# Two first blocks of a convolution and expert kernel brought in by VectorE products and TensorE sums, with the first loads in a new order

## The chip, the cores and the metric

The kernel runs on one core of one Trainium2 chip. The metric is the device time of one execution in microseconds, as the median over runs. The profile is one execution recorded by the hardware profiler; its span runs from the first to the last instruction.

## What is computed

The reference takes a sequence `x` of 2 x 4096 rows of 192 values and, for every row, 8 heads x 7 taps of weights. A softmax over the 7 taps weighs the row and its six predecessors; the result goes through two dense layers with a squared ReLU between them, and then through two more with `h * cos(h)` between them:

```python
w = exp(weight_gen - max); w = w / (sum(w) + 1e-09)          # over the 7 taps
out = einsum('bshk,bskhg->bshg', w, x_unf)                   # x_unf: 7 neighbouring rows, zeros ahead of a batch
h = np.maximum(out @ w_in, 0.0);  x2 = (h * h) @ w_out       # 192 -> 2048 -> 192
h = x2 @ w_in2;                   y  = (h * np.cos(h)) @ w_out2
```

All in fp32. The kernel splits each fp32 operand in a high and a low part (`hi`, `lo`) of a shorter format that TensorE multiplies fast, and adds three products.

## The kernel before, in words

**Tiling.** The 8192 rows are 16 blocks of 512. One block of one expert is 16 steps, one for each 128 of the 2048 hidden columns. A step has five first-layer matmuls of 512 columns (`first_product`, line 560, into a PSUM tile `h`, of which there are four), the nonlinearity and the split in `hi` and `lo` (`between`, lines 588 to 618), and five second-layer matmuls (`second_product`, lines 577 to 583, into `acc`), which come six steps later. 16 blocks, two experts, 16 steps each: 512 steps, 5120 such matmuls. The first two blocks of the first expert are interleaved: the first block goes `ALONE` steps by itself, then the steps of both alternate.

**The start.** Before the first step TensorE needs the first block's rows, weighed by the softmax, transposed and split, and the first expert's weights, split. `load_x(0)` (line 361) loads the first block in 128 partitions of ten rows (`xc`); the two first partitions, which reach ahead of the batch, come by two small loads, the others by a load of 62 partitions on SP's queue and one of 64 on ACT's. `softmax(0, 0, 1)` works on the weights `wgen` of this block. `first_x1` (line 469) multiplies rows and weights for one row in four at a time on VectorE (`product`, line 441, the tile `pr` of 7 taps x 192), sums the taps of the first 128 columns by seven matmuls with the identity, which also transpose (line 482), and those of the last 64 by three additions on VectorE (line 487, written to `twice`) and a transpose on TensorE (line 493). All other blocks go through `attend` (line 449: products on GpSimd, one reduction each on VectorE, line 454) and `x1` (line 500: a transpose on VectorE, then out to DRAM and back to finish it, then a split).

**The weights** of the first expert are converted in pieces by `weight` (line 274): a load, then operations on ACT, VectorE and GpSimd (lines 303 to 320) that rebuild the value exactly, and the split (lines 264 to 271). Pieces: `wiAhi`, `wiAlo` (first layer, first 128 of 192 rows), `wiB` (last 64) and `wo` (second layer).

**The order.** Nothing is issued where it is written. Each operation is put in a list with its possible engines and a cost, and `Order.issue` (line 112) lays the list out by due times and by its own guess of when data arrive (`SENT`, `RATE`, `SEEN` for loads; `since` keeps an operation from being placed too early). On the chip each engine then runs its instructions in that fixed order. `WARM` matmuls with the identity (line 700) run while TensorE would have nothing to do.

Of the kernel before, what the change touches and what calls it, by code (L numbers as in the profile page):

```python
# [10 lines left out]
F32 = mybir.dt.float32  # L11
F32R = mybir.dt.float32r
# [14 lines left out]
ALONE = 6  # L27
WARM = 16
# [27 lines left out]
class Order:  # L56
    WAIT = 0.14

    SENT, RATE, SEEN = 0.65, 360e3, 0.77
# [117 lines left out]
def conv_moe_kernel(  # L177
# [46 lines left out]
    def load(dst, out_fn, in_ap, size, key=None, reads=(), by=1e9, queue="sp"):  # L224
        op({queue: 0.45}, lambda e: eng[e].dma_start(out=out_fn(), in_=in_ap), reads=reads,
           writes=[(dst, key)], size=size, by=by)
# [47 lines left out]
    def weight(m, part, c0, n):  # L274
        name = f"{part}{m}_{c0}"
        by = -99.0 if m == c0 == 0 and part != "o" else 1e9
        if m == 0:
            order.since = 3.0 if by < 0 else 5.0
# [4 lines left out]
        if part == "a":  # L283
            cols = n
            load(raw, lambda: flat()[:, 0:2 * n], w_in[m][0:P, 2 * c0:2 * (c0 + n)], P * n * 8, by=by)
        elif part == "b":

            cols = n // 2
            ap = w_in[m][P:D, 2 * c0:2 * (c0 + n)].rearrange("d (j k c) -> k d j c", k=2, c=2 * P)
            for k in range(2):  # L290
                load(raw, lambda k=k: flat()[k * DB:(k + 1) * DB, 0:n].rearrange("d (j c) -> d j c", c=2 * P),
                     ap[k], DB * n * 4, key=k, by=by)
# [68 lines left out]
    def load_x(b):  # L361
# [10 lines left out]
        if b:  # L372
            load(t, lambda: flat(p0, P, 0), rows_of(p0, P), P * rows * D * 4, key="all")
        else:
            for n, q in enumerate(((p0, P // 2), (P // 2, P))):
                load(t, lambda q=q: flat(*q, 0), rows_of(*q), P // 2 * rows * D * 4, key=f"all{n}", by=-100.0,
                     queue="act" if n else "sp")
# [90 lines left out]

    def first_x1():
        t = [buf(ps, [P, N], F32, "h", 4, f"first{part}") for part in range(2)]  # L470
        for i in range(BS):
# [6 lines left out]
            there = lambda part, i=i: t[part].t.rearrange("d (p i) -> d i p", i=BS)[:, i]  # L478

            def taps(e, pr=pr, there=there):  # L480
                for k in range(K):
                    nc.tensor.matmul(there(0), lhsT=pr.t[:, k, 0:P], rhs=ident.t, start=k == 0, stop=k == K - 1)
            op({"pe": 0.24 * K}, taps, [ident, (pr, 0)], [(t[0], i)])

            def fold(e, pr=pr, twice=twice):
# [5 lines left out]
            op({"dve": dve(3 * DB) + 2 * dve(2 * DB)}, fold, [], [(pr, 1), twice])  # L491

            op({"pe": 0.24}, lambda e, twice=twice, there=there: nc.tensor.transpose(
                there(1), twice.t.rearrange("p q d -> p (q d)"), ident.t), [ident, twice], [(t[1], i)])
        for part in range(2):
            split((0, 0), part, t[part], True)

# [160 lines left out]
    for b in range(NB):  # L658
# [8 lines left out]
        when(ago(NF + 8), load_x, b)  # L667
        if b % CB == 0:
            c = b // CB
            if c == 1:  # L670
                when(ago(2 * NF - 6), load_g, c)
                when(ago(2 * NF - 9), softmax, c, 0, CB)
            else:
                n = 14 + 9 * c
                when(n, early_exp, c, 2.27 * n + START + 15)
                when(ago(2 * NF), late_softmax, c)
        when(ago(NF), attend, b)
# [16 lines left out]
    with tc.manual_schedule():  # L694
# [56 lines left out]
```

## Time and profile before

| | |
|---|---|
| median of 3 runs | 1278.64 us (1277.4 to 1281.92) |
| the profiled execution | 1277.48 us |
| its span, first to last instruction | 1274.5 us |
| TensorE's mean granted clock over the span | 0.981 |
| TensorE busy | 1196.8 us, 94% |
| ScalarE, VectorE, GpSimd busy | 83%, 71%, 43% |

The span is 3.0 us shorter than the execution's own time. Busy shares are means over a start in which weights are converted and a long steady part. In rows, PE is TensorE's matmuls, PEld its weight loads, DVE VectorE, ACT ScalarE, POOL GpSimd, and SPq or ACTq the instructions that issue DMAs; `L560` is a line of the kernel; the bracket at a row's end is idle time ahead of it and what ended it.

### The profile page before, as it was taken

What the parts mean: (1) busy time and instruction counts of PE and PEld (TensorE: products, weight loads), DVE (VectorE), ACT (ScalarE), POOL (GpSimd) and SP (SyncE); (2) the same over time, 40 slices, a digit from 0 to 9 for tenths busy, and PEclk for the clock granted to TensorE, in tenths of its full rate; (3) what the DMA queues carried; (4) which work ended last, traced back from release to release, by engine and by line L of the source; (5) the groups of instructions that cost most, each with busy time, mean ns of one, the idle gap of its engine ahead of it and who ended that gap; (6) DMA issues with size and microseconds to landing.
All of it is one profiled execution on the core that took longest, in us unless ns stands there. A gap on an engine that the chain in (4) does not pass through costs nothing.

```text
span 1274.5 us, 16270 instructions
## 1 busy us (share of the span) xinstructions
PE 1196.8 (94%) x5212; PEld 979.1 (77%) x5212; DVE 902.8 (71%) x1217; ACT 1054.9 (83%) x1992; POOL 551.2 (43%) x425
## 2 busy tenths in 40 slices
PE   4488999989999999999999999999999999999998
PEld 4367777778787887878788787878878888888886
DVE  5998879775958578585866758576674646777765
ACT  1486887869788797978879798888988979999996
POOL 3678465564615244260534526153332304444443
PEclk8689999999999999999999999999999999999999
DMA  4532435320212112021111202111020210111001
GB/s 115 154 96 67 133 109 166 113 69 21 80 30 69 25 31 79 10 72 31 56 46 28 74 9 69 34 37 27 24 47 9 54 30 13 30 30 30 13 7 19
DMA packets 91945, 68.67 MB, mean 54 GB/s; under 512 B 56020, under 2 KB 77268, under 8 KB 91860
## 3 DMA queue, kind: packets, MB, share of 16 engines
q1 hardware_dynamic: 91780, 67.16, 19.1%
q8 instruction: 40, 0.66, 0.2%
q10 hardware_dynamic: 80, 0.49, 0.2%
q14 instruction: 45, 0.37, 0.1%
HBM read 47.76 MB, written 19.86 MB: 53 GB/s over the span
## 4 chain that ended last, share of the span: by engine, by line
PE 50%; ACT 18%; DVE 14%; issue 5%; DMA 2%; POOL 1%; SPq 1%; DVEq 0%; ACTq 0%; POOLq 0%
PE h L560 25%; PE acc L579 5%; PE acc L577 5%; PE acc L578 5%; PE acc L582 5%; PE acc L583 5%; ACT hi L264 5%; DVE lo L271 4%; ACT rr L609 4%; ACT rr L610 4%; DVE g L612 2%; ACT kk L604 2%; DVE rr L607 2%; ACT g L598 2%; DVE at L454 1%
## 5 line engine op out<-in xcount | busy, mean ns | idle before, releaser
L271 POOL TENSOR_TENSOR lo<-g,hi 128x512 fp32r<-128x512 f32 x201 | 260.2, 1295 | 557.4 <-ACT hi L264 489.3
L271 DVE TENSOR_TENSOR lo<-g,hi 128x512 fp32r<-128x512 f32 x215 | 175.0, 814 | 157.1 <-ACT hi L264 147.5
L264 ACT ACTIVATE hi<-g 128x512 fp32r<-128x512 f32 x416 | 259.8, 625 | 1.9 <-DVE g L612 0.9
L607 DVE SCALAR_TENSOR_TENSOR rr<-kk,h 128x512 f32<-128x512 int32 x256 | 174.4, 681 | 90.0 <-ACT kk L604 90.0
L612 DVE TENSOR_TENSOR g<-h,rr 128x512 f32<-128x512 f32 x256 | 175.0, 684 | 38.6 <-POOL lo L271 26.8
L577 PE MATMUL acc<-hi,wo 128*128 128x512 f32 x512 | 200.3, 391 | 1.5 <-ACT wo L264 1.5
L578 PE MATMUL acc<-hi,wo 128*128 128x512 f32 x512 | 200.6, 392 | 1.0 <-DVE wo L271 1.0
L582 PE MATMUL acc<-lo,wo 128*128 128x512 f32 x512 | 200.4, 391 | 0.0
L579 PE MATMUL acc<-hi,wo 128*128 128x512 f32 x512 | 200.4, 391 | 0.0
L583 PE MATMUL acc<-lo,wo 128*128 128x512 f32 x512 | 200.2, 391 | 0.0
L594 ACT ACTIVATE rr<-h 128x512 f32<-128x512 f32 x256 | 150.7, 590 | 51.0 <-PE h L560 50.0
L609 ACT ACTIVATE rr<-rr 128x512 f32<-128x512 f32 x256 | 161.1, 629 | 27.7 <-DVE rr L607 27.4
L610 ACT ACTIVATE rr<-rr 128x512 f32<-128x512 f32 x256 | 161.2, 630 | 1.8
L604 ACT ACTIVATE kk<-h 128x512 int32<-128x512 f32 x256 | 151.1, 590 | 8.5 <-PE h L560 7.8
L598 ACT ACTIVATE g<-rr 128x512 f32<-128x512 f32 x160 | 100.7, 630 | 55.1 <-DVE lo L271 51.5
L441 POOL TENSOR_TENSOR pr<-xc,wgen_late 128x1344 f32<-128x1344 f32 x48 | 139.5, 2984 | 13.2 <-DVE at L454 11.8
L577 PEld LDWEIGHTS acc<-hi,wo 128*128 128x128 f32 x512 | 96.8, 189 | 22.1 <-ACT wo L264 1.9
L578 PEld LDWEIGHTS acc<-hi,wo 128*128 128x128 f32 x512 | 96.7, 189 | 21.6 <-DVE wo L271 1.3
L582 PEld LDWEIGHTS acc<-lo,wo 128*128 128x128 f32 x512 | 96.7, 189 | 20.3
L583 PEld LDWEIGHTS acc<-lo,wo 128*128 128x128 f32 x512 | 96.8, 189 | 20.1
L579 PEld LDWEIGHTS acc<-hi,wo 128*128 128x128 f32 x512 | 96.8, 189 | 20.0
L454 DVE TENSOR_REDUCE at<-pr 128x192 f32<-128x1344 f32 x60 | 92.3, 1539 | 0.0
(558 smaller groups left out, 2243.7 us busy)
## 6 DMA issues: line engine op xcount, KB each, us to landing
xc<-in_x_dram SPq DMA_DIRECT2D x14, 960.0 KB, 4.7
x2d<-x2a SPq DMA_DIRECT2D x16, 256.0 KB, 2.0
x<-x2d SPq DMA_DIRECT2D x32, 128.0 KB, 2.7
x<-x2d SPq DMA_DIRECT2D x16, 256.0 KB, 2.7
out_dram<-oa SPq DMA_DIRECT2D x64, 64.0 KB, 2.0
x1d<-xt SPq DMA_DIRECT2D x60, 64.0 KB, 1.8
x<-x1d SPq DMA_DIRECT2D x15, 256.0 KB, 2.7
x<-x1d SPq DMA_DIRECT2D x30, 128.0 KB, 2.6
```

What stands on the lines that cost most here:

```text
L264: nc.scalar.activation(out, in_, AF.Copy)
L271: eng[e].tensor_tensor(out=out, in0=in0, in1=in1, op=ALU.subtract)
L560: nc.tensor.matmul(h.t, lhsT=w.t[:, sl], rhs=v.t, start=n == 0, stop=n == len(ops) - 1)
L577: nc.tensor.matmul(o0.t, lhsT=w(0), rhs=hi.t, start=start, stop=False)
L578: nc.tensor.matmul(o1.t, lhsT=w(2), rhs=hi.t, start=start, stop=False)
L579: nc.tensor.matmul(o0.t, lhsT=w(1), rhs=hi.t, start=False, stop=False)
L582: nc.tensor.matmul(o1.t, lhsT=w(2), rhs=lo.t, start=False, stop=stop)
L583: nc.tensor.matmul(o0.t, lhsT=w(0), rhs=lo.t, start=False, stop=stop)
L607: op({"dve": dve(N)}, lambda e: nc.vector.scalar_tensor_tensor(out=r.t, in0=k.t, scalar=-TWO_PI, in1=h.t, op0=ALU.mult, op1=ALU.add), [k, ...
L609: op({"act": act(N)}, lambda e: nc.scalar.activation(r.t, r.t, AF.Abs), [], [r])
L610: op({"act": act(N)}, lambda e: nc.scalar.activation(r.t, r.t, AF.Sin, scale=-1.0, bias=math.pi / 2), [], [r], behind=exps if (b, f) == (0 ...
L612: op({"dve": dve(N)}, lambda e: nc.vector.tensor_tensor(out=g.t, in0=h.t, in1=r.t, op=ALU.mult), [h, r], [g])
```

## The change

Line numbers of the changed file stand about 30 higher from `between` on and a few higher before. What it does:

- The first block's load is one of 126 partitions on SP (and the two small ones); nothing of it is on ACT's queue.
- The three loads of the first weight pieces (`wiA` and `wiB` of the first columns) go on ACT's queue, behind the first exponential in ACT's order. The second block's load is recorded after the second half of the softmax, with `since` 6.5.
- The second block no longer goes through `attend` and `x1`: `second_slot` multiplies on VectorE and sums all 192 columns' taps by 14 matmuls with the identity, between steps of the first block; `second_x1` splits from PSUM (the last 64 rows twice, for both halves of the partitions).
- `ALONE` is 8 and not 6, `WARM` 26 and not 16; the planner's figures for loads and for the fold's cost are others.

```diff
-ALONE = 6
-WARM = 16
+ALONE = 8
+WARM = 26
...
-    SENT, RATE, SEEN = 0.65, 360e3, 0.77
+    SENT, RATE, SEEN = 0.75, 300e3, 0.8
...
+        early = dict(queue="act", behind=exps[:1], by=by) if by < 0 else {}
         if m == 0:
-            order.since = 3.0 if by < 0 else 5.0
+            order.since = 0.0 if by < 0 else 6.5
...
-        if b:
-            load(t, lambda: flat(p0, P, 0), rows_of(p0, P), P * rows * D * 4, key="all")
-        else:
-            for n, q in enumerate(((p0, P // 2), (P // 2, P))):
-                load(t, lambda q=q: flat(*q, 0), rows_of(*q), P // 2 * rows * D * 4, key=f"all{n}", by=-100.0,
-                     queue="act" if n else "sp")
+        if b == 1:
+            order.since = 6.5
+        load(t, lambda: flat(p0, P, 0), rows_of(p0, P), P * rows * D * 4, key="all", by=1e9 if b else -100.0)
+        order.since = 0.0
...
+    def second_slot(i):
+        if i == 0:
+            acc[0, 1] = [buf(ps, [P, N], F32, f"acc{part}", 2, f"second{part}") for part in range(2)]
+        t = acc[0, 1]
+        pr = sbuf([P, K, D], F32, "pr", 2, f"pr1_{i}")
+        product(1, i, pr, ways={"dve": dve(K * D)})
+        for part in range(2):
+            rows = slice(P, D) if part else slice(0, P)
+            op({"pe": 0.24 * K}, lambda e, pr=pr, rows=rows, there=slot(t[part], i): taps(
+                e, there(rows.stop - rows.start), pr, rows), [ident, pr], [(t[part], i)])
...
+        if b == 1:
+            for i in range(BS):
+                when(ALONE - 6 + i, second_slot, i)
+            when(ALONE - 2, second_x1)
+            continue
         when(ago(NF), attend, b)
         when(ago(10), x1, b)
...
         softmax(0, 1, CB)
+        load_x(1)
```

How the planner's order moves, at three places. **SP's queue at the start**, before and then in the change (`wgen` is the taps' weights, `xc` a block's rows, `wo_early` and `wiB_early` places in which the first raw weights are put):

```order
L225 DMA wgen_99<-in_weight_gen_dram 128x224
L225 DMA xc_101<-in_x_dram 62x1920
L225 DMA xc_101<-in_x_dram 1x768
L225 DMA xc_101<-in_x_dram 1x1536
L225 DMA wgen_99<-in_weight_gen_dram 128x224
L225 DMA xc_108<-in_x_dram 128x1920
L225 DMA wgen_112<-in_weight_gen_dram 128x224
L225 DMA wo_early<-in_moe_w_in_dram 128x512
```

```order
L225 DMA wgen_109<-in_weight_gen_dram 128x224
L225 DMA xc_111<-in_x_dram 126x1920
L225 DMA xc_111<-in_x_dram 1x768
L225 DMA xc_111<-in_x_dram 1x1536
L225 DMA wgen_109<-in_weight_gen_dram 128x224
L225 DMA wgen_117<-in_weight_gen_dram 128x224 x2
L225 DMA xc_134<-in_x_dram 128x1920
L225 DMA wo_early<-in_moe_w_in_dram 128x768
```

The first block's rows (`xc_101`, now `xc_111`) come as one load, and the first weight piece (`128x512`) has left this queue for ACT's.

**VectorE, from the first block's last fold to the first block's split**, before and then in the change (`at` is `attend`'s sum for the second block, `xlo_(0, 0)` the low part of the first block):

```order
L454 TENSOR_REDUCE at_200<-pr_0_174 128x192
L313 TENSOR_SCALAR wiB_early<-wo_early 128x256 x2
L487 TENSOR_TENSOR wo_early<-wo_early 128x3x64
L487 TENSOR_TENSOR wo_early<-wo_early 128x2x64
L487 TENSOR_TENSOR wo_early<-wo_early 128x128
L318 SCALAR_TENSOR_TENSOR wiB_early<-wiAlo_early,wiB_early 128x256 x2
L454 TENSOR_REDUCE at_200<-pr_1_198 128x192
L313 TENSOR_SCALAR wiB_early<-wo_early 128x384
L315 TENSOR_SCALAR wiAlo_early<-wiAlo_early 128x384
L271 TENSOR_TENSOR xlo_(0, 0)_224<-first_132,xhi_(0, 0)_203 128x512
```

```order
L491 TENSOR_TENSOR wo_early<-wo_early 128x3x64
L491 TENSOR_TENSOR wo_early<-wo_early 128x2x64
L491 TENSOR_TENSOR wo_early<-wo_early 128x128
L315 TENSOR_SCALAR wiB_early<-wo_early 128x256 x2
L320 SCALAR_TENSOR_TENSOR wiB_early<-wiAlo_early,wiB_early 128x256 x2
L402 TENSOR_REDUCE mx_1_214<-wgen_109 128x32
L271 TENSOR_TENSOR xlo_(0, 0)_216<-first_140,xhi_(0, 0)_202 128x512
```

The reductions of the second block and the next weight piece are gone from ahead of the first block's split.

**VectorE after the first tiles**, in the change (`pr_0_246` to `pr_2_308` are products of the second block, `lo_294` and `lo_327` the low parts of the first two steps):

```order
L441 TENSOR_TENSOR pr_0_246<-xc_134,wgen_109 128x1344
L271 TENSOR_TENSOR wiAlo_67<-wiB_early,wiAhi_65 128x384
L441 TENSOR_TENSOR pr_1_274<-xc_134,wgen_109 128x1344
L320 SCALAR_TENSOR_TENSOR wiB_early<-wiAlo_early,wiB_early 128x256
L271 TENSOR_TENSOR lo_294<-h_235,hi_276 128x512
L315 TENSOR_SCALAR wiB_early<-wo_early 128x384 x2
L441 TENSOR_TENSOR pr_2_308<-xc_134,wgen_109 128x1344
L320 SCALAR_TENSOR_TENSOR wiB_early<-wiAlo_early,wiB_early 128x384
L271 TENSOR_TENSOR lo_327<-h_249,hi_291 128x512
```

These products stood on GpSimd before; they now lie among the weights' operations on VectorE, between the first tiles.

## Rows read from the trace of the kernel before

**Rows 1.** The page: the span and the instructions in it.

```profile
span 1274.5 us, 16270 instructions
```

**Rows 2.** Timeline of PE: start, duration, instruction, idle time before it.

```profile
26.63 1.83 PE L482 MATMUL first<-ident,wo_early 128*128 128x128 f32 x14 [2.44 <-DVE wo_early L441]
...
45.66 0.79 PE L560 MATMUL h<-xlo_(0, 0)_224,wiAhi 128*128 128x512 f32 x1 [6.23 <-DVE wiB_early L318]
...
108.89 0.50 PE L560 MATMUL h<-xlo_(0, 1)_370,wiAhi 128*128 128x512 f32 x1 [1.56 <-DVE lo L271]
```

**Rows 3.** Chain of waits in order of time: start, length, what.

```profile
111.45 1.13 PE h L560 x5
```

**Rows 4.** Waits of PE, 0 to 120 us: total, times, longest.

```profile
PE first L482 <- DVE pr L441: 12.3, 1, 12.3
...
PE h L560 <- DVE wiB_early L318: 6.2, 1, 6.2
```

**Rows 5.** Windows: length, busy by engine, granted clock, DMA share, GB/s.

```profile
5.00:10.00 5.00, 1.94 (x17) 1.75 (x16) 0.63 (x2) 0.00 (x0) 0.00 (x0) 1.00 0.99 254
10.00:15.00 5.00, 0.00 (x0) 0.00 (x0) 0.00 (x0) 0.00 (x0) 0.00 (x0) 0.69 0.15 52
...
270.00:271.00 1.00, 1.00 (x6) 0.82 (x5) 1.00 (x3) 0.00 (x0) 1.00 (x2) 1.00 0.88 361
```

**Rows 6.** DMA issues: of 0 to 25 us, of 255 to 300 us, and the page's.

```profile
xc<-in_x_dram SPq DMA_DIRECT2D x1, 465.0 KB
...
xc<-in_x_dram SPq DMA_DIRECT2D x1, 945.0 KB
...
xc<-in_x_dram SPq DMA_DIRECT2D x14, 960.0 KB, 4.7
```

**Rows 7.** Timeline of the queues and of ACT, same columns as rows 2.

```profile
1.19 1.36 SPq L225 DMA_DIRECT2D xc<-in_x_dram  x3
3.83 0.39 ACT L404 ACTIVATE wgen<-wgen 128x224 f32<-128x224 f32 x1 [1.59 <-DVE wgen L403]
21.67 0.44 ACT L303 ACTIVATE wiAlo_early<-wo_early 128x256 f32<-128x256 f32 x1 [17.46 <-DMA wo_early<-in_moe_w_in_dram]
...
267.34 0.67 SPq L225 DMA_DIRECT2D xc<-in_x_dram  x2
```

**Rows 8.** Timeline of DVE and POOL at the start.

```profile
5.27 0.39 DVE L414 TENSOR_TENSOR wgen<-wgen,sx 128x224 f32<-128x224 f32 x1
17.61 3.03 DVE L441 TENSOR_TENSOR pr<-xc,wgen 128x1344 f32<-128x1344 f32 x2 [11.94 <-DMA xc<-in_x_dram]
25.02 5.39 DVE L441 TENSOR_TENSOR wo_early<-xc,wgen 128x1344 f32<-128x1344 f32 x2
25.24 7.67 POOL L441 TENSOR_TENSOR pr<-xc,wgen 128x1344 f32<-128x1344 f32 x2 [0.39 <-DVE wgen L414]
35.08 2.90 DVE L313 TENSOR_SCALAR wiB_early<-wo_early 128x256 uint32<-128x256 uint32 x2
```

**Rows 9.** One line's instructions, 0 to 110 us: duration ns min/median/max, first and last start.

```profile
L441 DVE TENSOR_TENSOR pr<-xc,wgen x2: 1550/1554/1559, 17.6 to 19.1; 128x1344 f32<-128x1344 f32 x2
L487 DVE TENSOR_TENSOR wo_early<-wo_early x6: 291/291/2715, 30.3 to 38.6; 128x128 f32<-128x128 f32 x4, 128x192 f32<-128x192 f32 x2
L313 DVE TENSOR_SCALAR wiB_early<-wo_early x14: 282/480/2702, 35.1 to 99.2; 128x384 uint32<-128x384 uint32 x11, 128x256 uint32<-128x256 uint32 x3
L318 DVE SCALAR_TENSOR_TENSOR wiB_early<-wiAlo_early,wiB_early x18: 411/559/981, 38.8 to 100.5; 128x384 uint32<-128x384 uint32 x12, 128x256 uint32<-128x256 uint32 x6
L454 DVE TENSOR_REDUCE at<-pr x6: 1535/1539/1544, 33.6 to 108.8; 128x192 f32<-128x1344 f32 x6
```

**Rows 10.** Timeline of DVE at the end of the first weights.

```profile
96.73 2.84 DVE L313 TENSOR_SCALAR wiB_early<-wo_early 128x384 uint32<-128x384 uint32 x2
...
108.16 0.68 DVE L271 TENSOR_TENSOR lo<-h,hi 128x512 fp32r<-128x512 f32 x1
```

**Rows 11.** Windows of PE: length, busy (matmuls), granted clock, DMA share, GB/s.

```profile
250.00:270.00 20.00, 14.91 (x57) 0.91 0.11 36
```

More of the change, by code (lines that the diff above doesn't have):

```diff
@@ L222, in const, with load @@
         return Buf(None, tile=sb.tile(shape, dtype, name=name))
-    def load(dst, out_fn, in_ap, size, key=None, reads=(), by=1e9, queue="sp"):
+    def load(dst, out_fn, in_ap, size, key=None, reads=(), by=1e9, queue="sp", behind=None):
         op({queue: 0.45}, lambda e: eng[e].dma_start(out=out_fn(), in_=in_ap), reads=reads,
-           writes=[(dst, key)], size=size, by=by)
+           writes=[(dst, key)], size=size, by=by, behind=behind)
     ident = const([P, P], F32, "ident")
@@ L284, in weight @@
             cols = n
-            load(raw, lambda: flat()[:, 0:2 * n], w_in[m][0:P, 2 * c0:2 * (c0 + n)], P * n * 8, by=by)
+            load(raw, lambda: flat()[:, 0:2 * n], w_in[m][0:P, 2 * c0:2 * (c0 + n)], P * n * 8, **early)
         elif part == "b":
@@ L291, in weight @@
                 load(raw, lambda k=k: flat()[k * DB:(k + 1) * DB, 0:n].rearrange("d (j c) -> d j c", c=2 * P),
-                     ap[k], DB * n * 4, key=k, by=by)
+                     ap[k], DB * n * 4, key=k, **early)
         else:
@@ L466, in split, with taps, slot @@
         xs[key, part] = hi, lo
+    def taps(e, there, pr, rows):
+        for k in range(K):
+            nc.tensor.matmul(there, lhsT=pr.t[:, k, rows], rhs=ident.t, start=k == 0, stop=k == K - 1)
+    def slot(t, i):
+        return lambda rows=P: t.t[0:rows].rearrange("d (p i) -> d i p", i=BS)[:, i]
     def first_x1():
@@ L477, in first_x1 @@
             product(0, i, pr, ways={"dve": dve(K * D)})
[L478 to L483, printed above, removed]
+            op({"pe": 0.24 * K}, lambda e, pr=pr, there=slot(t[0], i): taps(e, there(), pr, slice(0, P)),
+               [ident, (pr, 0)], [(t[0], i)])
             def fold(e, pr=pr, twice=twice):
@@ L490, in fold, with second_x1 @@
                 add(twice.t, *(p[:, k].unsqueeze(1).to_broadcast([P, 2, DB]) for k in range(2)))
-            op({"dve": dve(3 * DB) + 2 * dve(2 * DB)}, fold, [], [(pr, 1), twice])
-            op({"pe": 0.24}, lambda e, twice=twice, there=there: nc.tensor.transpose(
-                there(1), twice.t.rearrange("p q d -> p (q d)"), ident.t), [ident, twice], [(t[1], i)])
+            op({"dve": 1.0}, fold, [], [(pr, 1), twice])
+            op({"pe": 0.24}, lambda e, twice=twice, there=slot(t[1], i): nc.tensor.transpose(
+                there(), twice.t.rearrange("p q d -> p (q d)"), ident.t), [ident, twice], [(t[1], i)])
         for part in range(2):
             split((0, 0), part, t[part], True)
+    def second_slot(i):
[8 more added lines that the diff above has]
+                e, there(rows.stop - rows.start), pr, rows), [ident, pr], [(t[part], i)])
+    def second_x1():
+        t = acc.pop((0, 1))
+        split((0, 1), 0, t[0], True)
+        hi = sbuf([P, N], F32R, "xhi1", 2, "xhi1_second")
+        lo = sbuf([P, N], F32R, "xlo1", 2, "xlo1_second")
+        for k in range(2):
+            q = slice(k * DB, (k + 1) * DB)
+            op({"act": act(N, True)}, lambda e, q=q: copy(e, hi.t[q], t[1].t[0:DB]), [t[1]], [(hi, k)])
+            op({"dve": dve(N)}, lambda e, q=q: sub(e, lo.t[q], t[1].t[0:DB], hi.t[0:DB].bitcast(F32)),
+               [t[1], (hi, 0)], [(lo, k)])
+        xs[(0, 1), 1] = hi, lo
     def x1(b):
@@ L666, in conv_moe_kernel @@
         ago = lambda n: max(t - n, -1) if b > 1 else -1
-        when(ago(NF + 8), load_x, b)
+        if b > 1:
+            when(ago(NF + 8), load_x, b)
         if b % CB == 0:
```

## The prediction

> **What bounds the kernel now.** Start with the span [rows 1] and the work TensorE has to do in it. In the chain of waits five first-layer matmuls take 1.13 us [rows 3], so a step, with its second five, takes 2.27 us and the 512 steps 1161 us. The span is 1274.5 us; about 113 us are start, waits and tail. Where they lie is read from TensorE's timeline [rows 2]: the first of these matmuls starts at 45.66 us, and the 22nd first-layer tile at 108.89 us. By then 21 first-layer fives and 15 second-layer fives are done, 36 x 1.13 = 40.8 us of work, so 68 of the 113 us are lost ahead of this point. From here TensorE is nearly always fed. The change touches what lies ahead of it, and I take the start of the 22nd tile as the mark: the same 36 fives precede it in the changed order.
>
> Two things hold TensorE up ahead of the mark. **First, the rows of the first block are late.** Its first wait is 12.3 us for VectorE's product [rows 4], which itself waits 11.94 us for a DMA and starts at 17.61 us, though the softmax was done at 5.66 [rows 8]. The windows show why: from 5 to 10 us the DMA engines are full (share 0.99, 254 GB/s), from 10 to 15 the share is 0.15, at 52 GB/s [rows 5]. That is about two engines of 16 finishing something: the load of 62 partitions, 465 KB [rows 6]. The same load for the first block of the second batch has 126 partitions and 945 KB [rows 6], is issued at 267.34 us [rows 7], and moves at 361 GB/s with a share of 0.88, that is 14 engines of 16 [rows 5].
>
> **Second, VectorE and GpSimd stand in each other's way.** A product alone takes 1.55 us [rows 9], but the pair that starts at 25.02 takes 5.39 us while GpSimd's pair, begun at 25.24, takes 7.67 [rows 8]. A fold of 0.29 us at its shortest takes 2.72 at its longest, a scalar operation 0.28 and 2.70; a reduction takes 1.54 us always [rows 9]. To measure this I add VectorE's instructions at the shortest time from the start of each form to the next one's start (product 1.55, fold 0.35 + 0.28 + 0.29, scalar operation 0.27 or 0.34, two-operand 0.38 or 0.54, split of a tile 0.60, reduction 1.54, and so on). From the first product (17.61) to the first matmul the 33 instructions add to 18.8 us and take 28.0; the 88 from there to the split at 108.16 that the 22nd tile waits for [rows 10] add to 43.7 us and take 63.2, a factor of 1.45. VectorE has hardly any idle time there, so it sets the pace.
>
> **The change, part by part.**
>
> *Arrival of the first block.* Issue at 1.19 us [rows 7]; a load of this size lands 4.7 us after its issue in the median of 14 [rows 6], so 5.9 us; 112 KB of softmax weights ahead of it and as much behind cost up to 0.9 us at 254 GB/s [rows 5]. I take 6.8, against 17.61: 10.8 us earlier. The ends are 5.9 and 8.8 (below, fourth rival). The softmax's 5.66 us does not delay it.
>
> *From there to the first matmul.* The changed order has four products 6.2, four folds 3.7, the first two weight pieces 1.3, a maximum 0.4 and the split 0.6: 12.2 us. The first weights land well before: their issue moves from behind the late load to behind the exponential that starts at 3.83 us [rows 7], where they were first used at 21.67. One more us goes to GpSimd's share of the first pieces: first matmul at 6.8 + 12.2 + 1.0 = 20.0 us, 25.7 us earlier than 45.66. The rest of the gain over the arrival comes from what is no longer ahead: GpSimd's products, two reductions, a softmax half, the next weight piece.
>
> *From the first matmul to the mark.* This stretch grows. In the changed order VectorE has here 90 instructions of 48.3 us, 4.6 more than before: four products of the second block (+6.2), a softmax half (+2.1), a weight piece that stood ahead (+1.3), a reduction and a square more (+2.2), less two reductions (-3.1), two transposes (-1.7) and some weight operations that the planner now gives to other engines (-2.4). At the factor of 1.45 that is 70.0 us, 6.8 more than 63.2. The mark comes at 90.0 us, 18.9 earlier. The factor is the least certain term: 14 instructions of 7.0 us took 7.4 from 17.61 to 25.02 [rows 8], a factor of 1.06; ten of 5.8 us took 11.4 from 96.73 to 108.16, beside GpSimd's products [rows 10], a factor of 1.96. I take the one of the same stretch, since most of its work is the same.
>
> *What lies beside.* The 56 extra matmuls with the identity come in eight groups of seven; a group takes 1.83 us [rows 2], 14.6 us in all. They lie between the first tiles, where TensorE waits for weights: until the second block joins it has 12 fives, 13.6 us, and these, in the some 35 us that VectorE needs to get there. Ten more warm matmuls end near 10.4 us (5.6 us for 16 before), ahead of the fourth product at about 14. The second block's eleven DMAs by way of DRAM go away, its splits from PSUM add two small operations, and the second block joining two tiles later moves steps without adding any. Each costs nothing as long as VectorE sets the pace; without that cover the groups are the second rival.
>
> *After the mark* the order of VectorE hardly differs, block for block, so the waits stay as they are and the rest shifts whole.
>
> **Sum:** -10.8 - 14.9 + 6.8 = -18.9 us. The profiled execution took 1277.48 us, 1.2 below the median; 1277.5 - 18.9 = **1258.6 us**. What follows the end does not change.
>
> **Rivals.**
>
> 1. *VectorE and GpSimd get further into each other's way (slower).* The second block's four products now stand on VectorE between weight operations that GpSimd's next operation waits for, and each in turn waits for what GpSimd has begun, as at 25.02 [rows 8]. If the stretch to the mark ran at the factor 1.96, it would take 94.7 us, the mark would come at 114.7 and the time be 1283.3. It decides from a factor of 1.84, where nothing is gained. For it: the products are long two-operand instructions. Against it: GpSimd loses four such products of its own in this part. The Trainium skill ("SBUF — State Buffer", Who interferes with whom) says that a VectorE instruction with two SBUF inputs and a GpSimd instruction that reads SBUF hold the shared ports whole, the other one blocking fully. By that rule the new products cost more than their 6.2 us; the pair of rows at 25 us agrees with it.
>
> 2. *TensorE becomes the bound of the start.* If VectorE ran near its shortest times, the mark would wait for 20.0 + 40.8 + 14.6 = 75.4 us: 33.5 us earlier, 1244.0. For it: GpSimd's first products are gone. Against it: the factor from 45 to 108 us had few of them in it.
>
> 3. *A later stretch gives part of it back.* From 250 to 270 us VectorE was overfull and TensorE did 57 matmuls [rows 11] where 20 us hold 88, 7.0 us lost. Blocks 2 to 5 keep their work but not its exact order; a second such stretch gives 1265.6.
>
> 4. *The weights' loads get in the way of the first block's.* Three loads of 512 KB in all on ACT's queue are issued near 4.2 us, before the first block has landed. If all 1690 KB to be moved by then shared the 254 GB/s [rows 5], the rows would come at 2.0 + 6.8 = 8.8 us: 1260.6. The Trainium skill ("DMA: Bandwidth & Descriptors", Issuing engines are not separate DMA queues) says that loads from different engines end up on the same 16 DMA engines and interleave. By that rule the second queue hides nothing, and this change would lose these 2 us.
>
> 5. *The first load stays slow.* If 945 KB went at 52 GB/s [rows 5], they would take 18.6 us and land near 19.8: 13.0 us later than I say, 1271.6. The load at 267 us speaks against it.
>
> **How the numbers follow.** The forecast has 0.55, with its own range from factors of 1.3 to 1.6: 62.8 to 77.3 us, times of 1251.4 to 1265.9. Rival 2 has 0.15, rival 3 0.12, rival 4 0.10, rival 5 0.03 and rival 1 0.05, of which 0.02 fall near no change. The range reaches into the second rival and past the third and fourth: 1247 to 1269. A measurement can tell about 0.3%, 3.8 us, from no change. Faster by more: 0.55 + 0.15 + 0.12 + 0.10 + 0.03 = 0.95, of which I take 0.01 off for two of the losses together; same 0.03, slower 0.03.
>
> **What would show it.** In the changed profile the first product should start at 6 to 9 us, the first first-layer matmul at 18 to 23, and the 22nd first-layer tile at 83 to 97; no GpSimd product before VectorE's splits of about the 13th tile; and the distance from the mark to the end should be 1165.6 us as now, within 5. A first product after 15 us would show the fifth rival; a mark at 75 to 80 us with TensorE always busy ahead of it the second; a mark after 105 the first. A longer distance from the mark to the end would show the third, and mean that the steady part does depend on what the start leaves behind, which this prediction denies.

## The result and the profile after

The changed kernel took 1264.09 us in the median of four runs (1260.91 to 1265.01), the kernel before 1278.02 in the four runs beside it: a ratio of 0.988, 95% interval 0.985 to 0.991. The forecast was 1258.6, the range 1247 to 1269. The profiled execution took 1264.08 us, 13.4 less than the 1277.48 of before. Of these, 12.2 lie in the span and 1.2 in what lies around it (1.8 us instead of 3.0), which the forecast had left as it was.

The span, from the page:

```profile
span 1262.3 us, 16521 instructions
```

The first block's rows, the first matmul and the mark, in the timelines of VectorE and TensorE, answer to [rows 2] and [rows 8]:

```profile
8.63 3.03 DVE L441 TENSOR_TENSOR pr<-xc,wgen 128x1344 f32<-128x1344 f32 x2 [3.02 <-DMA xc<-in_x_dram]
```

```profile
21.73 0.50 PE L587 MATMUL h<-xlo_(0, 0)_216,wiAhi 128*128 128x512 f32 x1 [1.78 <-ACT wiAhi L264]
...
28.28 3.50 PE L471 MATMUL second<-ident,pr 128*128 128x128 f32 x28 [1.20 <-DVE pr L441]
...
57.88 0.79 PE L587 MATMUL h<-xlo_(0, 0)_216,wiAhi 128*128 128x512 f32 x1 [6.45 <-DVE lo L271]
58.47 0.63 PE L587 MATMUL h<-xhi_(0, 0)_202,wiAlo 128*128 128x512 f32 x1
...
95.92 0.39 PE L587 MATMUL h<-xlo_(0, 1)_449,wiAhi 128*128 128x512 f32 x1
```

Against before, the first product comes 8.98 us earlier, the first first-layer matmul 23.93, the mark 12.97. From the mark to the end of the span it is 1262.3 - 95.92 = 1166.4 us, where before had 1165.6. So the span's gain is all made ahead of the mark, and nearly half of what the first matmul won is given back on the way: 74.2 us from it to the mark instead of 63.2. The row at 57.88 is new. TensorE stands still for 6.45 us ahead of the ninth tile and then runs its matmuls in 0.63 us instead of 0.39, at a granted clock of 0.50 from 57.9 to 60 us, the lower of the two levels (1.2 GHz).

TensorE's waits up to 120 us answer to [rows 4]: 12.3 and 6.2 us are gone, the two largest left are these.

```profile
PE h L587 <- DVE lo L271: 10.5, 4, 6.4
PE h L587 <- ACT wiAhi L264: 1.8, 1, 1.8
```

The windows of [rows 5] and [rows 11] (columns as there) now read:

```profile
5.00:10.00 5.00, 5.00 (x37) 5.00 (x36) 1.94 (x3) 0.00 (x0) 0.00 (x0) 1.00 0.96 224
10.00:15.00 5.00, 4.11 (x34) 3.68 (x34) 4.93 (x7) 0.88 (x2) 4.11 (x4) 1.00 0.73 270
```

```profile
250.00:270.00 20.00, 18.94 (x81) 14.67 (x80) 15.58 (x19) 15.56 (x30) 15.41 (x14) 1.00 0.35 108
```

The stretch at 10 to 15 us with two DMA engines of 16 is gone. The thin stretch at 250 to 270 us has only moved with the rest: the 40 us from 215.9 hold 134 matmuls, where before's lowest 40 us, from 228.9, held 146; against that, the 40 us from 295.9 are full (178), where before had 164 at 308.9. What the first stretch loses (12 matmuls, some 2.7 us) the second makes good.

The first GpSimd product is this one. Eleven tiles have begun by then, and VectorE has split seven; the forecast had named the splits of about the 13th:

```profile
65.95 3.05 POOL L441 TENSOR_TENSOR pr<-xc,wgen 128x1344 f32<-128x1344 f32 x1
```

### The profile page after: what moved, and what is told of

It is laid out like the page before. It is cut to its first block, busy times and chain, and to the rows that moved or that the text cites. A ratio compares the mean times of both kernels' runs of the same rounds, so it can differ in the third digit from the quotient of the medians.

```text
span 1262.3 us, 16521 instructions
## 1 busy us (share of the span) xinstructions
PE 1210.8 (96%) x5344; PEld 993.8 (79%) x5344; DVE 897.4 (71%) x1212; ACT 1057.5 (84%) x1988; POOL 547.6 (43%) x430
## 4 chain that ended last, share of the span: by engine, by line
PE 62%; DVE 16%; ACT 14%; issue 4%; DMA 1%; POOL 1%; SPq 1%; DVEq 0%; POOLq 0%; ACTq 0%
PE h L587 31%; PE acc L604 6%; PE acc L606 6%; PE acc L605 6%; PE acc L610 6%; PE acc L609 6%; ACT hi L264 4%; ACT rr L636 3%; ACT rr L637 3%; DVE lo L271 3%; DVE g L639 2%; ACT kk L631 2%; DVE at L454 2%; DVE rr L634 2%; ACT g L625 1%
## 5 line engine op out<-in xcount | busy, mean ns | idle before, releaser
L271 POOL TENSOR_TENSOR lo<-g,hi 128x512 fp32r<-128x512 f32 x197 | 255.4, 1297 | 557.6 <-ACT hi L264 518.6
L271 DVE TENSOR_TENSOR lo<-g,hi 128x512 fp32r<-128x512 f32 x219 | 178.8, 816 | 159.8 <-ACT hi L264 151.7
L454 DVE TENSOR_REDUCE at<-pr 128x192 f32<-128x1344 f32 x56 | 86.3, 1541 | 0.1
```

The source lines that it names most:

```text
L271: eng[e].tensor_tensor(out=out, in0=in0, in1=in1, op=ALU.subtract)
```

## The experiments

The theory after the result: the arrival of the rows passes through in full; from the first product to the mark VectorE sets the pace, stretched by GpSimd beside it. The rivals: the new wait at 51 to 58 us is made by one instruction in ACT's order; or TensorE itself, which has no gap from 28 to 51 us, is the bound because of the taps. All runs in one table (us; "way" is from the first product to the mark, from each run's trace; time is the median, ratio against the kernel before in the same runs):

| run | first product | first matmul | mark | way | mark to end | time | ratio, 95% |
|---|---|---|---|---|---|---|---|
| before | 17.61 | 45.66 | 108.89 | 91.3 | 1165.6 | 1278.02 | |
| changed | 8.63 | 21.73 | 95.92 | 87.3 | 1166.4 | 1264.09 | 0.988 (0.985 to 0.991) |
| e1_one_load | 9.82 | 38.01 | 101.84 | 92.0 | 1166.4 | 1269.51 | 0.992 (0.991 to 0.994) |
| e2_two_loads | 17.80 | 30.62 | 104.76 | 87.0 | 1166.0 | 1273.72 | 0.995 (0.994 to 0.997) |
| e3_second_by_gpsimd | 9.17 | 40.08 | 97.75 | 88.6 | 1170.9 | 1273.97 | 0.996 (0.995 to 0.998) |
| e4_softmax_later | 8.52 | 21.62 | 94.38 | 85.9 | 1166.3 | 1262.01 | 0.986 (0.985 to 0.987) |
| e5_changed_again | 8.93 | 22.01 | 94.47 | 85.5 | 1164.2 | 1260.58 | 0.986 (0.984 to 0.988) |
| e6_weights_after_rows | 8.13 | 21.16 | 95.79 | 87.7 | 1163.8 | 1261.97 | 0.987 (0.985 to 0.988) |
| e7_one_tap | 9.01 | 22.12 | 96.70 | 87.7 | 1167.2 | 1264.74 | 0.989 (0.987 to 0.990) |
| e8_one_tap_small_product | 8.33 | 21.44 | 92.64 | 84.3 | 1167.3 | 1260.73 | 0.985 (0.983 to 0.987) |
| e9_quarter_additions | 8.72 | 21.77 | 89.57 | 80.9 | 1167.3 | 1256.92 | 0.981 (0.979 to 0.984) |
| e10_no_fold | 8.59 | 27.89 | 92.07 | 83.5 | 1144.6 | 1238.45 | 0.967 (0.965 to 0.969) |
| e11_old_figures | 9.12 | 22.29 | 93.74 | 84.6 | 1164.3 | 1258.58 | 0.983 (0.981 to 0.985) |
| e12_late_split_on_gpsimd | 9.11 | 22.21 | 96.31 | 87.2 | 1146.3 | 1244.38 | 0.971 (0.969 to 0.974) |

Three runs have the changed kernel's order unaltered up to the mark (changed, e5, e12): their ways are 87.3, 85.5 and 87.2, their first products 8.63, 8.93 and 9.11. So a way is known to about 1 us either side of 86.7, and an arrival to a few tenths; what the ways differ by is told with e5. Two parts of the change have no run of their own: the ten more warm matmuls, and `ALONE` at 8, which e3 takes back together with the second block's move.

### The load alone, and undone

e1 is the kernel before with one load; e2 the changed kernel with two again:

```diff
-        if b:
-            load(t, lambda: flat(p0, P, 0), ...)
-        else:
-            for n, q in enumerate(((p0, P // 2), (P // 2, P))):
-                load(t, lambda q=q: flat(*q, 0), ..., queue="act" if n else "sp")
+        load(t, lambda: flat(p0, P, 0), ..., by=1e9 if b else -100.0)
```

> The kernel before with one part of the change alone: the first block's rows as one load of 126 partitions instead of two of 62 and 64. Theory (the gain is made of the arrival and of what no longer stands on VectorE ahead of the first matmul, and the two add): first product at 7 to 9 us instead of 17.61, everything behind it earlier by the same 9 to 10.5 us, mark near 99, time 1267 to 1269. Rival A (the start is bound by the weights' path, so the rows' arrival hardly counts): first product at 7 to 9, but the first matmul earlier by less than 4 us and the time above 1273. Rival B (two loads were as fast, something else kept the rows): first product still after 15 us, time 1278.

> The changed kernel with the first block's rows in two loads again, 62 partitions on SP and 64 on ACT's queue. Theory (the parts add): first product back at about 17.6 us, 9 us later than the 8.63 of the changed kernel, first matmul at about 30.7, mark at about 104.9, time 1273. Rival (VectorE does the weights' pieces while it waits, so that the wait is partly covered): first product at 17.6, mark only 3 to 5 us later than 95.92, time 1267 to 1269.

In e1 the rows come 7.8 us earlier and the mark 7.05; the way is that of before (92.0 and 91.3). In e2 the rows come 9.17 us later and the mark 8.84; the way is that of the changed kernel. The theory holds in both directions: what the arrival wins or loses, the mark wins or loses but for 0.3 to 0.7 us, and neither the weights' path nor work done in the meantime covers it. e1's rows came at 9.82, later than the 7 to 9 expected. In that run the second block's 960 KB (issued at 2.99 us) and two loads of weights (from 4.00 us) were already on their way beside them.

### The second block by GpSimd again

```diff
-ALONE = 8
+ALONE = 6
...
-        if b == 1:
-            for i in range(BS):
-                when(ALONE - 6 + i, second_slot, i)
-            when(ALONE - 2, second_x1)
-            continue
```

> The changed kernel with the second block done as before: products on GpSimd, sums and transposes on VectorE, through DRAM, joining at tile 6. Theory (moving it off GpSimd is what shortens the way from the first product to the first matmul): first product at 8 to 9 us, then 25 to 28 us to the first matmul instead of 13.1, so a first matmul at 33 to 37; from there to the mark about 63 us as in the kernel before; mark at 97 to 100, time 1266 to 1269. Rival (the second block's products only put 4.6 us more work on VectorE, which sets the pace): mark 3 to 5 us earlier than 95.92, time 1259 to 1261.

GpSimd's products are back ahead of the first matmul, which comes 18 us later:

```profile
16.56 7.68 POOL L441 TENSOR_TENSOR pr<-xc,wgen 128x1344 f32<-128x1344 f32 x2 [2.40 <-DVE wgen L414]
26.56 2.64 POOL L441 TENSOR_TENSOR pr<-xc,wgen 128x1344 f32<-128x1344 f32 x1 [2.32 <-DVE at L454]
```

```profile
40.08 0.80 PE L587 MATMUL h<-xlo_(0, 0)_232,wiAhi 128*128 128x512 f32 x1 [9.91 <-ACT wiAhi L264]
```

The first matmul came at 40.08, 3 us later than expected, yet the mark only 1.8 us later than the changed kernel's; the way is 88.6 against 86.7. The median was 5 us above what I expected; the profiled execution, the fastest of the five, took 1270.41. Against the changed kernel's profile that is 6.3 us more, of which 1.8 lie ahead of the mark and 4.5 behind it (1170.9). So moving the second block off GpSimd, with its later joining, brings the first matmul forward by 18 us and gives nearly all of it back before the mark: 1.4 to 3.3 us are left against the three runs of the unaltered order. More of what it is worth here lies behind the mark, where the planner then orders blocks 2 to 5 otherwise (153 matmuls in the 40 us from 137.8, where the changed kernel has 164 from 135.9). Why that order is worse stays open.

### One instruction in ACT's order

```diff
-                when(ago(2 * NF - 9), softmax, c, 0, CB)
+                when(ago(2 * NF - 9), later_softmax, c, 52.0)
...
+    def later_softmax(c, since):
+        order.since = since
+        softmax(c, 0, CB)
+        order.since = 0.0
```

> The changed kernel with one edit: the maximum, difference, exponential and division of the third and fourth blocks' softmax are released by the planner from 52 us of its time on instead of about 31 (its own estimate, the trace runs some 12 us behind it). ACT's order is the same up to the splits of the second block, and the exponential no longer stands there. Theory (the 6.45 us for which TensorE waits at 51 to 58 us come from ACT standing 3.05 us in front of that exponential with the squares and splits of tiles 5 to 8 behind it): this wait shrinks to 1 to 3 us, TensorE keeps its full clock there, the mark comes at 90 to 92 and the time is 1258 to 1261. Rival (VectorE's sum of work sets the pace, the wait only moves to the next tiles): mark within 1.5 us of 95.92, time 1263 to 1265. A loss beyond 1266 would mean that the third block's products now come late for its first tile.

In the changed kernel ACT stands in front of the exponential of the third and fourth blocks, and VectorE's split of the fifth tile, which frees the buffer for the ninth, comes at 57.15:

```profile
51.51 0.58 ACT L404 ACTIVATE wgen<-wgen 128x448 f32<-128x448 f32 x1 [3.05 <-DVE wgen L403]
...
55.44 0.59 ACT L264 ACTIVATE hi<-h 128x512 fp32r<-128x512 f32 x1
```

In e4 ACT has the tile's upper part ready at 51.90, 3.5 us earlier, but VectorE's split follows only at 55.45, in the place that its own order gives it:

```profile
51.90 0.60 ACT L264 ACTIVATE hi<-h 128x512 fp32r<-128x512 f32 x1
```

```profile
54.42 1.10 DVE L320 SCALAR_TENSOR_TENSOR wiB_early<-wiAlo_early,wiB_early 128x256 uint32<-128x256 uint32 x2
55.45 0.68 DVE L271 TENSOR_TENSOR lo<-h,hi 128x512 fp32r<-128x512 f32 x1
```

```profile
56.18 0.80 PE L587 MATMUL h<-xlo_(0, 0)_216,wiAhi 128*128 128x512 f32 x1 [4.85 <-DVE lo L271]
```

The wait shrinks by 1.6 us, to 4.85, where 1 to 3 were expected, and the way (85.9) is within what the unaltered order shows; e5, the changed kernel itself, has the same ratio. The wait on ACT is real, but behind it stands VectorE, and nothing measurable is won.

> The changed kernel itself, as the yardstick of the three runs beside it: 1262 to 1266 us, mark at 95.9, stall of 6.4 us ahead of the ninth tile.

It took 1260.58, 1.4 us less than expected. The wait ahead of the ninth tile was there (6.40 us), but the mark came at 94.47, 1.5 us earlier than in the first profile, with VectorE's order unaltered. The two traces part at TensorE's clock. Both runs have the lower level after the wait at 51 to 58 us. After a shorter wait the changed kernel's first profile has it once more, and e5 has not (TensorE's first matmul after this wait, and the window from 72 to 74 us, first profile and then e5):

```profile
71.91 0.69 PE L587 MATMUL h<-xlo_(0, 0)_216,wiAhi 128*128 128x512 f32 x1 [2.09 <-DVE lo L271]
```

```profile
72.00:74.00 2.00, 2.00 (x5) 1.61 (x6) 2.00 (x4) 0.00 (x0) 2.00 (x4) 0.51 0.00 0
```

```profile
72.05 0.50 PE L587 MATMUL h<-xlo_(0, 0)_216,wiAhi 128*128 128x512 f32 x1 [1.98 <-DVE lo L271]
```

```profile
72.00:74.00 2.00, 1.95 (x9) 1.61 (x10) 2.00 (x3) 0.49 (x1) 2.00 (x4) 1.00 0.00 0
```

In the first profile ACT and then VectorE wait there for the slower matmuls. e12 (mark at 96.31) has this second stretch too, as have e6, e7 and e8; e9, e10 and e11 have not, so their marks are to be held against the 94.47 of e5.

### The weights' loads behind the rows

```diff
+            def after_rows():
+                if early:
+                    nc.scalar.activation(seen.t[64:P], xc[0].t[64:P, 0, 0:1], AF.Copy)
+                return flat()[:, 0:2 * n]
```

> The changed kernel with one instruction more on ACT: ahead of its three early weight loads it copies one column of the first block's rows, so these 512 KB are not asked for before the rows have landed. No engine's order changes otherwise. Theory (the loads share the transfer, the fourth rival): first product 1.5 to 2 us earlier, at 6.6 to 7.1 us instead of 8.63, and everything behind it too; mark at 94, time 1.5 to 2 us below the changed kernel's in the same runs. Rival (the 945 KB and the softmax weights around them take this long by themselves: in the run with one load alone, where the weights stood on SP's queue, the rows came no earlier, at 9.82): first product at 8.0 to 9.0, time within 1 us. It would lose if the first weights came too late for the first tile: they are due by about 17 us.

The first product came at 8.13, where e5 beside it has 8.93 and the nine other runs with these loads in the changed kernel's order lie from 8.33 to 9.17 (8.81 in the mean of the ten). So by this one execution the 512 KB cost the rows some 0.7 us (0.2 to 1.0), not 2, and nothing clear of the spread reached the mark (95.79); the weights were first used at 11.12 instead of 10.39. The fourth rival's mechanism is there at about a third of its price. What else keeps the rows until 8.1 was not tried. Behind them SP issues three loads of softmax weights of 112 KB, of which the forecast had counted one. Two of them go out ahead of the rows' landing; the third stands on SP's queue until the rows have landed and goes out at 8.46 (queues of SP and ACT, what SP waits for, and the third load, changed kernel):

```profile
2.59 6.20 SPq L225 DMA_DIRECT2D wgen<-in_weight_gen_dram  x3
```

```profile
3.77 1.76 ACTq L225 DMA_DIRECT2D wo_early<-in_moe_w_in_dram  x3
```

```profile
SPq L225 <- DMA xc<-in_x_dram: 5.0, 1, 5.0
```

```profile
8.46 0.33 SPq L225 DMA_DIRECT2D wgen<-in_weight_gen_dram  x1
```

### The taps

```diff
-        for k in range(K):
+        for k in range(n):
...
-            op(..., lambda ...: taps(e, there(rows.stop - rows.start), pr, rows), ...)
+            op(..., lambda ...: taps(e, there(rows.stop - rows.start), pr, rows, 1), ...)
```

> The changed kernel, which for the second block sums only the first of the seven taps on TensorE (six taps' matmuls left out, so the second block's rows are not the reference's); VectorE's products and every other order stay. A slot's group goes from 3.4 us to about 0.5, 11.7 us less work on TensorE between 28 and 51 us. Theory (VectorE's work sets the pace up to the mark, TensorE only waits in other places): the tiles 3 to 8 come earlier, the wait ahead of the ninth tile grows by nearly as much, mark at 94 to 96, time 1262 to 1265. Rival (TensorE, without a gap from 28 to 51 us, is the bound there): mark at 84 to 91, time 1253 to 1259.

The window from 28.3 to 51.3 us, of the changed kernel and of e7:

```profile
28.30:51.30 23.00, 23.00 (x152) 19.96 (x152) 22.87 (x28) 14.10 (x30) 19.97 (x23) 1.00 0.50 146
```

```profile
28.30:51.30 23.00, 17.06 (x56) 11.92 (x56) 22.88 (x29) 14.54 (x31) 20.10 (x22) 0.75 0.46 146
```

Of TensorE's 152 matmul records 56 are left, and VectorE's and GpSimd's columns are the same. The eighth tile came some 1 us earlier, the wait ahead of the ninth grew to 7.5 us, and the mark came at 96.70, no earlier than the 94.5 to 96.3 of the unaltered order. The taps cost nothing, though TensorE had no gap beside them: the rival falls. The fewer matmuls even ran at a lower clock (0.75 granted instead of 1.00).

### VectorE's products, and GpSimd's additions

e8 also cuts VectorE's four products to the one tap; e9 cuts GpSimd's additions instead:

```diff
-        product(1, i, pr, ways={"dve": dve(K * D)})
+        product(1, i, pr, ways={"dve": dve(K * D)}, n=1)
```

> As the run with one tap, and VectorE's four products of the second block also cut to that tap (192 of 1344 elements a row; six taps left out of the second block), about 0.3 us instead of 1.5 to 1.9 each, 5.5 to 6.2 us less work on VectorE ahead of the mark; every order stays. Theory (VectorE's work sets the pace, 1.45 us of time for 1 us of its work): mark 5.5 to 9 us earlier than with one tap alone. Rival (the pace is set by the chain through ACT, GpSimd and TensorE): mark within 2 us of the run with one tap.

The four took 7.66 us in e7 (1.85, 1.89, 2.09, 1.83) and 2.31 in e8. The way went from 87.7 to 84.3: 3.4 us for 5.35 us of VectorE's work, and the mark itself came 4.1 us earlier, less than the 5.5 expected and more than the rival's 2. With a way known to about 1 us, that is 0.4 to 0.8 us of time for one of VectorE's work, not 1.45. VectorE's work sets the mark, but only in part; the rest ends as waiting for others.

```diff
-        op({"pool": pool(cols)}, lambda e: nc.gpsimd.tensor_tensor(out=st(), in0=st(), in1=vt(), op=ALU.add), [v], [sg])
+        part4 = lambda t: t()[:, 0:cols // 4] if m == 0 else t()
+        op({"pool": pool(cols)}, lambda e: nc.gpsimd.tensor_tensor(out=part4(st), in0=part4(st), in1=part4(vt), op=ALU.add), [v], [sg])
```

> The changed kernel in which GpSimd adds the low halves of the first network's weights only to the first quarter of each piece's columns (three quarters of these additions are left out, so those weights miss their low bits). Every engine's order stays. Between the first matmul and the mark these 17 additions took 16.4 us of GpSimd's time, of 49 us in instructions with two operands in memory; about 11 us of them go. VectorE's instructions there take some 20 us longer in all than at their shortest. Theory (VectorE's instructions are stretched by GpSimd's two-operand instructions beside them, as in the first rival): the stretching falls by 4 to 5 us, VectorE's 128x384 scalar_tensor_tensor (958 ns in the mean) and tensor_scalar (710 ns) come down to 650 to 850 and 500 to 620 ns, the mark comes 4 to 6 us earlier, at 89 to 91. Rival (the stretching has another cause, such as waits inside VectorE): the means stay within 8%, the mark within 1.5 us of 94.5 to 95.9.

VectorE's groups by form from the first matmul to the mark (busy us, mean ns of one), of the kernel before, the changed kernel and e9:

```profile
L318 DVE SCALAR_TENSOR_TENSOR wiB_early<-wiAlo_early,wiB_early 128x384 uint32<-128x384 uint32 x11 | 7.8, 717 | 0.1
```

```profile
L320 DVE SCALAR_TENSOR_TENSOR wiB_early<-wiAlo_early,wiB_early 128x384 uint32<-128x384 uint32 x12 | 11.5, 958 | 0.0
...
L315 DVE TENSOR_SCALAR wiB_early<-wo_early 128x384 uint32<-128x384 uint32 x11 | 7.7, 710 | 0.1
```

```profile
L315 DVE TENSOR_SCALAR wiB_early<-wo_early 128x384 uint32<-128x384 uint32 x11 | 8.1, 755 | 0.1
L320 DVE SCALAR_TENSOR_TENSOR wiB_early<-wiAlo_early,wiB_early 128x384 uint32<-128x384 uint32 x12 | 8.0, 667 | 0.0
```

GpSimd's additions fell from 16.4 to 7.0 us, the mark came 4.9 to 6.7 us earlier than in the three runs of the unaltered order (4.9 against e5, whose clock went the same way), and VectorE's two-operand form came down from 958 to 667 ns, as expected. The scalar form did not (710 to 755, where 500 to 620 were expected). VectorE's busy time from the first matmul to the mark (third figure after the length) fell by 7.2 us, in the same instructions, in the changed kernel and e9:

```profile
21.73:95.92 74.19, 61.49 (x292) 49.17 (x293) 69.32 (x91) 50.13 (x101) 58.72 (x67) 0.91 0.27 82
```

```profile
21.77:89.57 67.80, 60.42 (x293) 48.68 (x293) 62.16 (x91) 49.71 (x101) 48.46 (x66) 0.92 0.28 90
```

By the forecast's count this work takes 48.3 us at its shortest, so a third of the 21 us of stretching went with 9.4 us of GpSimd's additions. The edit also shortens the weights' own path through GpSimd; the run does not tell how much of the 5 us at the mark is that.

### The first block without folds

```diff
-            op({"pe": 0.24 * K}, ... taps(e, there(), pr, slice(0, P)), [ident, (pr, 0)], [(t[0], i)])
-            def fold(e, pr=pr, twice=twice):
-                ...
-            op({"dve": 1.0}, fold, [], [(pr, 1), twice])
-            op({"pe": 0.24}, ... nc.tensor.transpose(there(), ...), [ident, twice], [(t[1], i)])
+            for part in range(2):
+                rows = slice(P, D) if part else slice(0, P)
+                op({"pe": 0.24 * K}, ... taps(e, there(rows.stop - rows.start), pr, rows), [ident, pr], [(t[part], i)])
```

> The changed kernel in which the first block too is summed wholly on TensorE, as the second is: the four folds of VectorE (0.92 us each at their shortest) and the four transposes go, 28 more matmuls of 64 columns and one small split on ACT and on VectorE come. VectorE has 3.0 us less work ahead of the mark, TensorE some 5.8 us more ahead of the first matmul. Theory (VectorE's work sets the mark, at the 0.8 us of time for 1 us of its work that the small products showed): first matmul later, at 23 to 27 us, and yet the mark 2 to 3 us earlier than the 94.5 to 95.9 of the changed kernel, time 1258 to 1261 where the changed kernel has 1260.5 to 1264. Rival (the first matmul's delay passes on): mark 2 to 4 us later, time 1263 to 1267.

Ahead of the mark it went as the theory says, but for a first matmul that came a little later than the 23 to 27 expected: at 27.89, 6 us behind the changed kernel's. The mark came 2.4 to 4.2 us earlier (2.4 against e5). But the time is 1238.45, some 20 us below the expectation, and those lie behind the mark: 1144.6 us to the end. In the changed kernel TensorE waits at the first tile of each of the blocks 7 to 14, 16.5 us in all; in before it is much the same (16.1). At block 7, in the timelines of GpSimd, VectorE and TensorE:

```profile
389.42 5.78 POOL L441 TENSOR_TENSOR pr<-xc,wgen_late 128x1344 f32<-128x1344 f32 x2
```

```profile
392.64 3.05 DVE L271 TENSOR_TENSOR xlo_(0, 7)_3905<-x,xhi_(0, 7)_3892 128x512 fp32r<-128x512 f32 x1
```

```profile
395.75 0.50 PE L587 MATMUL h<-xlo_(0, 7)_3905,wiAhi 128*128 128x512 f32 x1 [2.68 <-DVE xlo_(0, 7)_3905 L271]
```

The split takes 3.05 us, though the same form takes 0.68 where GpSimd does nothing beside it (block 7's other split, at 359.19); it ends 0.5 us after the second of the two products, as it does, to within 0.1 us, in each of these eight blocks. In e10 the planner gave this split to GpSimd itself, between two products:

```profile
379.98 2.92 POOL L441 TENSOR_TENSOR pr<-xc,wgen_late 128x1344 f32<-128x1344 f32 x1
383.45 1.30 POOL L271 TENSOR_TENSOR xlo_(0, 7)_3901<-x,xhi_(0, 7)_3895 128x512 fp32r<-128x512 f32 x1 [0.56 <-ACT xhi_(0, 7)_3895 L264]
384.71 3.35 POOL L441 TENSOR_TENSOR pr<-xc,wgen_late 128x1344 f32<-128x1344 f32 x1
```

> The changed kernel with the planner's old figures for transfers and for the fold; all else stays, TensorE's and most of the early order too. Theory (these figures only reshuffle instructions that VectorE does anyway): mark within 2 us of 94.5 to 95.9, time 1260 to 1266. Rival (the figures are a part of the gain): mark 3 us later or more, time above 1267.

e11 takes back the planner's figures (SENT, RATE, SEEN and the fold's cost): way 84.6, time 1258.58, nothing lost. The new figures are no part of the gain.

### The late split alone

```diff
-        op({"dve": dve(N)} if psum else {"dve": dve(N), "pool": pool(N)},
+        op({"dve": dve(N)} if psum else {"pool": pool(N)} if part == 0 and key[0] == 0 and key[1] > 6 else {"dve": dve(N), "pool": pool(N)},
```

> The changed kernel with one edit far behind the mark: the subtraction that splits the upper 128 rows of the blocks 7 to 15 on their way into the first network may only go to GpSimd (the planner could choose, and chose VectorE in the changed kernel, GpSimd in the run without folds). Up to about 350 us every order is the changed kernel's. In the changed kernel this instruction takes 3.05 us on VectorE beside a pair of GpSimd's products (0.68 us alone), and TensorE waits for it at the first tile of each of the blocks 7 to 14: 1.8 to 2.7 us each, 16 to 17 us in all. Theory (the run without folds won its 20 us behind the mark by this choice alone): no such wait is left, mark at 94 to 96 as in the changed kernel, 1146 to 1150 us from the mark to the end instead of 1164 to 1166, time 1241 to 1247. Rival (it won them by something that the start leaves behind, such as the clock or the buffers' turn): mark to end above 1158 us, time above 1254.

TensorE's waits behind 115 us, in the changed kernel (first rows) and in e12:

```profile
PE h L587 <- DVE lo L271: 10.6, 10, 3.7
PE h L587 <- DVE xlo_(0, 7)_3905 L271: 2.7, 1, 2.7
PE h L587 <- DVE xlo_(0, 11)_6927 L271: 2.4, 1, 2.4
```

```profile
PE h L587 <- DVE lo L271: 11.1, 11, 3.7
PE h L587 <- POOL xlo_(0, 14)_9185 L271: 0.2, 1, 0.2
PE h L587 <- POOL xlo_(0, 7)_3909 L271: 0.2, 1, 0.2
```

Mark at 96.31 (0.3 later than expected), 1146.3 us to the end, 1244.38 us: as the theory had it. The choice of engine for one instruction a block is worth 18 to 20 us behind the mark, and the start's own speed has no part in that. 15.9 us of it are the waits at the first tiles (16.5 before, 0.6 now). The planner answered the edit with moves of its own behind it (eight other splits went from GpSimd to VectorE), and the mean granted clock rose from 0.988 to 0.992; what share of the rest is whose was not separated. e10 has this and the shorter way, and at 1238.45 us it is the fastest kernel of the study, 0.967 of before.

## Why the prediction was right, and where its sizes were off

- **Arrival** (forecast 6.8, ends 5.9 and 8.8): 8.63. That one load brings the rows some 9 us earlier, and that the gain passes to the mark but for 0.3 to 0.7 us, was right (e1, e2). The size was 1.8 us off. The forecast let 112 KB of softmax weights behind the rows share with them; two such loads and the weights on ACT's queue were there, and the rest stays open. The Trainium skill ("DMA: Bandwidth & Descriptors", Issuing engines are not separate DMA queues) says that loads of different engines interleave on the same 16; by that rule the second queue hides nothing, and e6 agrees, at some 0.7 us in one execution.
- **First product to first matmul** (12.2 + 1.0 us): 13.1. Right, and by the path forecast: VectorE's twelve or so us, then GpSimd's addition and ACT's split of the first weights.
- **First matmul to mark** (70.0 us): 74.2 in the profiled run, 72.5 in e5. This is the term that was mis-sized. The step was to charge 48.3 us of VectorE's work at the factor of before, 1.45; it came to 1.54 (1.50 in e5). Two things make the difference. VectorE was busy for 69.3 us, 1.44 times its shortest, where before it was busy for 60.2 of 63.2 us, 1.38 times: some 2.8 us of the 4.2. Its two-operand form of the weights, 128x384, shows where: 717 ns in the mean before, 958 now (twelve of them, 2.9 us), 667 with shorter GpSimd additions beside it (e9). The other 1.5 us are idle time, and e5, without the second stretch of low clock, lacks 1.7: a term that the forecast did not have. A factor taken from one mix of work does not carry to another in which more two-operand work of both engines stands together. This is the first rival's mechanism, far from its 1.84.
- **What the two together mean.** The forecast had the second block's move win 14.9 us at the first matmul and lose 6.8 after it. It won 15.0 and lost 11.0, so 4.0 of the 13.0 us at the mark; e3 against the unaltered order puts it, with `ALONE`, at 1.4 to 3.3. The arrival alone makes the other 9.
- **Taps hidden** (14.6 us at nothing): right (e7), though not for lack of work on TensorE but because tiles that come earlier only wait longer ahead of the ninth. The second rival falls.
- **After the mark** (1165.6 us, unchanged): 1166.4. Right for this change, though in part by luck: the third rival's thin stretch lost some 2.7 us more than before, and another stretch gave it back. The reason given, that the steady part does not depend on what the start leaves behind, is wrong in general: e3 lost 4.5 us there and e10 won 20. For e10 the cause is shown (e12): the planner chose another engine for one instruction a block. That its estimates had shifted with the start is the likely reason for the choice and was not shown; for e3 the cause stays open.
- **Fifth rival:** fell with the first row of the profile.

The sum was -10.8 - 14.9 + 6.8 = -18.9; measured, -9.0 - 15.0 + 11.0 = -13.0 at the mark, +0.8 behind it, and -1.2 outside the span.

## What to carry to other kernels

Take a load's arrival out of a start first: here it passed through but for 0.7 us, while a matmul that starts 18 us earlier may give it all back where another engine sets the pace. Where VectorE and GpSimd share the work, count both engines' two-operand instructions together, and look for short instructions that last several times their shortest beside a long one. And compare not only the part that was changed: a planner that picks engines by small differences of its estimates can move 20 us at the other end of the program.

## What was not expected of the hardware

- One 128x512 subtraction on VectorE took 3.05 us beside GpSimd's products and 0.68 alone, and ended just after the product did. The Trainium skill ("SBUF — State Buffer", Who interferes with whom) calls the contention of the two engines' shared ports an exclusive lock, where the blocked one waits. The rows at 389 to 396 us agree: the second product ends at 395.20, the subtraction at 395.69. e12 shows what it cost, eight times 1.8 to 2.7 us on TensorE.
- Fewer matmuls, lower clock: with six of seven taps left out TensorE was granted 0.75 instead of 1.00 from 28 to 51 us, and the mark came no earlier (96.70; the changed kernel 95.92, and 94.47 in e5).
- After the 6.45 us wait the matmuls took 0.63 us, at the lower of the two clocks (granted 0.50). After a wait of some 2 us at 70 to 72 us the clock was at the lower level in the changed kernel's first profile (granted 0.51) and at the full one in e5 (1.00), with one order of instructions; their marks lie 1.5 us apart.
